# Routed attention and two feed-forward stages: number copies moved to the last products, four output buffers at first, a joined pair of tiles, another PSUM bank

## Chip, cores and metric

One NeuronCore of one Trainium2 chip. The metric is device time in microseconds; the median of three runs of the kernel before is 1136.23 us (1136.13 to 1136.47).

## What is computed

Three stages, all in float32 accuracy (4 batches, 8 heads, 576 tokens, head size 64; 2304 tokens of 512 features):

```python
scores = scale * np.matmul(q, k.transpose(0, 1, 3, 2))      # keep the 32 largest of each row
attn = softmax over the kept scores; x = attn @ v            # 2304 x 512
logits = xn @ en.T / tau; expert_idx = argmax                # 8 experts
out[mask] = gate_w * (relu(x[mask] @ w1[e]) @ w2[e])         # w1 512 x 1024, w2 1024 x 512
h = out @ w_in                                               # 512 x 2048
y = (relu(h) + alpha * min(h, 0)) @ w_out                    # 2048 x 512
```

## The kernel before, in words

The program is written out by hand: each engine (TensorE is PE, VectorE DVE, ScalarE ACT, GpSimd POOL, and SyncE SP, which issues nearly all transfers) executes its instructions in the order in which the code names them.

**Attention** (to about 466 us of the span) works on tiles of 128 queries. Of its eight PSUM banks one, `own`, holds small words (row sums, logits, gates); two hold the tiles `pt0`, into which PE transposes; five hold scores and outputs. `drain` puts work for the next stage between the last attention tiles: the splits of the first six weight units of the first expert, the transposes of its first 216 tokens, and three of its eight hidden tiles ("ahead"). Then `batch_done` routes the last batch: DVE computes logits, the place of each token (`place`, lines 708 and 709, reads the counts from a `pt0` tile) and the gates (`gates`, 690 and 691, read `own`), and POOL scatters the tokens' rows, sorted by expert, to `xs` in DRAM, with the token's number in column 512.

**Experts** (`run`, to about 733 us): nine blocks of tokens, two of the first expert and one of each other. A block has eight hidden tiles (`hidden`, 12 matmuls each) and then four column tiles `dc` of 24 matmuls. A float32 product is three fp32r products (`mm3`, lines 1098 to 1100) of high and low halves. So every weight unit (512 KB, a `raw` buffer of four, filled by an SP transfer) is split: ACT copies it, rounded, into `wt` (line 1022), and DVE or POOL subtracts (1023). `tick` does one item of a list of such splits and sends loads three items ahead; w_in and w_out, which are float64, are converted by `wide` on DVE and POOL in between. `turn` transposes the rows of the next block with PE (`x_chunk`, 1090, two `xt` banks), and ACT and DVE split them (1092, 1093). `gate` (1082) scales those rows by their gate first. A finished column tile is copied to `y` (two buffers, 1236 and 1238) and stored to `yt`. For each block but the first, `load_rows` also copies the block's token numbers, 4 bytes each, from column 512 of `xs` to `idc` with an SP transfer (line 1071, DRAM to DRAM).

**Last products** (`last_products`): nine groups of 256 tokens, passed twice (k = 0 to 17), once for each half of the 2048 features. Each k computes eight feature tiles f0 to f7 (12 matmuls each) and mixes them (`MIXED`) with seven products of the group before, by a seven-product scheme for a 2 x 2 block matrix; k = 0 has no products in between. At f7 `halves` splits the next group's columns (1268, 1269). Products are stored to `yp` in the first pass and scattered to the output in the second, by the numbers read back from `idc`. `Experts.bank` gives six PSUM banks, `mm`; in the experts and the last products they and the two `xt` banks lie on the attention's banks.

Of the kernel before, what the change touches and what calls it, by code (L numbers as in the profile page):

```python
# [48 lines left out]
class Attention:  # L49
    def __init__(self, ctx, tc, q, k, v, sb, ident):  # L50
# [8 lines left out]
        self.new_po()  # L59
        self.new_s()  # L60

        self.bank = self.ps.tile([P, 512], F32, name="own")
# [444 lines left out]
class Router:  # L507
# [161 lines left out]
    def batch_done(self, b):  # L669
# [89 lines left out]
        if b == B - 1:  # L759
# [3 lines left out]
                lambda: self.last_dots(3), numbers] + ahead(2) + [last_copies, root] + first + [  # L763
                counts, lambda: self.splits.pop(0)()] + [low[f] for f in range(AHEAD) if AT[f] == 1] + norm + [exps] + ahead(3) + [
                low[f] for f in range(AHEAD) if AT[f] == 2] + [place]
# [100 lines left out]
GAT = 4  # L866
EARLY_POOL = (0, 2, 4, 5)
RANKS = (0, 0, 16, 0, 0, 0, 0, 13)
ROWS = (-1, 0, 1, 2, 3, 4, 5)
GAT0, XAT0 = 0, ((), (), (), (), (0, 1), (2,), (3,), ())  # L870
XAT = ((), (0, 1), (), (2, 3), (), (), (), ())
# [4 lines left out]
class Experts:  # L876
# [3 lines left out]
    def __init__(self, tc, w1, w2, w_in, w_out, wa, xp, ident, xs, yt, idc, yp, ro, out):  # L880
        self.tc, self.nc = tc, tc.nc
        self.w1, self.w2, self.w_in, self.w_out = w1, w2, w_in, w_out
        self.ident, self.xs, self.yt, self.idc, self.out = ident, xs, yt, idc, out
        self.ro, self.wa, self.xp, self.yp = ro, wa, xp, yp
        self.W, self.rv = {}, {}
        self.items, self.sent = [], 0
        self.h0, self.p0, self.behind, self.ahead_of = [], [], [], []
        self.columns = None

# [31 lines left out]
    def early(self, lent):  # L921
# [4 lines left out]
        for k in range(EARLY):  # L926
            self.fetch(raws[k], k)
        return [lambda k=k: self.split(k, raws[k]) for k in range(EARLY)]

# [127 lines left out]
    def load_rows(self, r, o, n):  # L1057
# [11 lines left out]
        if r or o:  # L1069
            src = self.xs[ds(e * NT + o, n), DM]  # L1070
            self.after(4, lambda: nc.sync.dma_start(ids.rearrange("(a b) -> a b", a=8),
                                                    src.rearrange("(a b) -> a b", a=8)))
        else:
# [73 lines left out]
    def run(self, ctx, alpha):  # L1147
# [36 lines left out]
        for i, (r, o, n) in enumerate(blocks):  # L1184
# [40 lines left out]
            for dc in range(4):  # L1225
                ps = self.bank()[:, :n]
                for f in range(8):
                    u = self.W[8 * r + 4 + f // 2]
                    c = slice((f % 2) * 512 + dc * P, (f % 2) * 512 + (dc + 1) * P)
                    self.mm3(ps, u[:, 0, c], u[:, 1, c], hT[f][:, 0, :n], hT[f][:, 1, :n], f == 0, f == 7)  # L1230
                    if f == 3:
                        self.tick(2 * dc, 8)
                        turn(2 * dc)
                y = self.wk.tile([P, 512], F32, name="y", bufs=2)
                if dc % 2:
                    nc.scalar.activation(y[:, :n], ps, AF.Copy)
                else:
                    nc.vector.tensor_copy(y[:, :n], ps)
                self.after(2, lambda r=r, o=o, n=n, dc=dc, y=y, base=base: self.put(r, nc.sync.dma_start(
                    self.yt[dc, :, ds(base + o, n)] if r else self.yt[dc, :, o:o + n], y[:, :n])))  # L1240
                self.tick(2 * dc + 1, 8)
                if nb:
                    if i == 0 and dc == GAT0:
                        for j in range(4):
                            self.gate(rows[0], j)
                    turn(2 * dc + 1)
            xT, rows = nx, rows[1:]
        self.last_products(xT, len(plan[-2]), len(plan[-1]))
# [24 lines left out]
    def last_products(self, t, n0, n1):  # L1273
# [19 lines left out]

        def first(k, t, f):
            h, g = divmod(k, ng)
            ps = self.bank()[:, :G2]
            fs = slice(f * P, (f + 1) * P)
            for d in range(4):
                w = self.V[d]
                self.mm3(ps, w[:, 0, fs], w[:, 1, fs], t[d][:, 0, :G2], t[d][:, 1, :G2], d == 0, d == 3)  # L1300
            gg = G[k % 2][f // 4][:, f % 4]
# [3 lines left out]
        def weights(k, f):  # L1305
            self.n = n1 if k else n0
            full = 8 * (ng - 2) if k else 6
            at = 8 * (k - 1) + f if k else f
            for at in {6: (-1,), 7: (at - 1, at)}.get(f, (at,)) if k else (at,):
# [12 lines left out]
        def sums(k):  # L1322
# [4 lines left out]
            v.tensor_tensor(a11, a12, s2, op=OP.subtract)  # L1327
            return s2

        def fetch(k, tt):  # L1330
# [92 lines left out]
        for k in range(last + 1):  # L1423
# [3 lines left out]
            for s in order:  # L1427
# [7 lines left out]
                f = int(s[1])  # L1435
                first(k, t, f)
                if f == 7:
                    if k < last:
                        t = self.halves(x)
                        x = self.load_columns((k + 2) % ng if k + 2 <= last else ng)  # L1440
                    s2 = sums(k)
                    if k == last:
                        split(6, s2, v)
                for action in RENEW.get((k, f), ()):
                    action()
                if k and f < 5:
                    m, i, j = ((6, 0, 0), (5, 1, 0), (4, 1, 1), (2, 0, 1), (3, 0, 0))[f]
                    split(m, s2 if m == 6 else quarter(p, i, j))
                if f == 0 and not k:
                    nc.sync.dma_start(ids, self.idc[:NT].rearrange("(t p) -> p t", p=P))  # L1450
                if f == 1 and k == 1:
                    v.tensor_copy(idi, ids)
                if f == 3:
                    split(1, quarter(k, 0, 0))
                if f == 4:
                    s3 = new()
                    v.tensor_tensor(s3, quarter(k, 0, 0), quarter(k, 1, 0), op=OP.subtract)  # L1457
                if f == 5:
                    split(7, s3)
# [271 lines left out]
def tile_kernel(ctx, tc, q, k, v, emb, tau, w1, w2, w_in, w_out, alpha, out):  # L1731
# [11 lines left out]
    with ExitStack() as c0:  # L1743
        wa = c0.enter_context(tc.tile_pool(name="wa", bufs=1))
        xp = c0.enter_context(tc.tile_pool(name="xp", bufs=1))
        with ExitStack() as c1:
# [33 lines left out]
            def ahead(f):  # L1780
# [3 lines left out]
                if f < AHEAD:  # L1784
                    ex.ahead(f, banks[f])
            banks, ro.ahead, ro.low_half, ro.splits = [], ahead, ex.ahead_low, splits

            def drain(i):

                if i == -9:  # L1790
# [3 lines left out]
                    splits.extend(ex.early(lent))  # L1794
                if i >= 1 and len(splits) > 1:
                    splits.pop(0)()
# [42 lines left out]
```

## Time and profile before

| | |
|---|---|
| median of 3 runs | 1136.23 us |
| the profiled execution: time, span | 1134.85 us, 1133.0 us |
| PE busy | 1071.7 us (95%) |
| DVE / ACT / POOL busy | 78% / 64% / 67% |
| DMA | 134.99 MB, mean 119 GB/s |
| mean granted TensorE clock | 0.990 |

A busy PE is not PE at its best, but where PE is idle or its clock is granted at half, the time can be read off directly: the timeline gives, for each instruction that had to wait, the idle time before it and what ended it. Clock 1.00 is 2.4 GHz, 0.50 is 1.2 GHz.

### The profile page before, as it was taken

What the parts mean: (1) busy time and instruction counts of PE and PEld (TensorE: products, weight loads), DVE (VectorE), ACT (ScalarE), POOL (GpSimd) and SP (SyncE); (2) the same over time, 40 slices, a digit from 0 to 9 for tenths busy, and PEclk for the clock granted to TensorE, in tenths of its full rate; (3) what the DMA queues carried; (4) which work ended last, traced back from release to release, by engine and by line L of the source; (5) the groups of instructions that cost most, each with busy time, mean ns of one, the idle gap of its engine ahead of it and who ended that gap; (6) DMA issues with size and microseconds to landing.
All of it is one profiled execution on the core that took longest, in us unless ns stands there. A gap on an engine that the chain in (4) does not pass through costs nothing. (4 is left out here: it accounts for less than half of the span.)

```text
span 1133.0 us, 27513 instructions
## 1 busy us (share of the span) xinstructions
PE 1071.7 (95%) x9529; PEld 1019.0 (90%) x9529; DVE 884.8 (78%) x3443; ACT 724.2 (64%) x1543; POOL 759.8 (67%) x810
## 2 busy tenths in 40 slices
PE   4999999989998998998999999999999999999996
PEld 3888888878887887998999999999999999999996
DVE  7999999989998999644567566687999988556555
ACT  5999999999999989543445555453333455344341
POOL 4999988999899988514344445344665696675674
PEclk8999999999999999899999999999999999999999
DMA  6455343443343324188677888223333212311301
GB/s 176 129 148 152 97 103 100 116 116 80 96 105 94 68 53 169 44 198 219 205 200 195 211 240 245 83 68 117 127 94 114 74 47 66 103 66 57 122 30 41
DMA packets 149531, 134.99 MB, mean 119 GB/s; under 512 B 95054, under 2 KB 117582, under 8 KB 149382
## 3 DMA queue, kind: packets, MB, share of 16 engines
q1 hardware_dynamic: 145942, 123.16, 40.2%
q0 software_dynamic: 2912, 9.46, 2.3%
q8 instruction: 77, 1.26, 0.5%
q14 instruction: 72, 0.59, 0.2%
q10 hardware_dynamic: 528, 0.52, 0.1%
HBM read 89.82 MB, written 33.92 MB: 109 GB/s over the span
## 5 line engine op out<-in xcount | busy, mean ns | idle before, releaser
L1099 PE MATMUL mm<-xT,wt 128*128 128x256 f32 (+7 forms) x852 | 246.9, 290 | 3.4 <-DVE xT L1269 2.2
L1098 PE MATMUL mm<-xT,wt 128*128 128x256 f32 (+7 forms) x852 | 246.3, 289 | 3.4 <-DVE xtail L691 1.4
L1100 PE MATMUL mm<-xT,wt 128*128 128x256 f32 (+7 forms) x852 | 245.9, 289 | 0.0
L301 POOL TENSOR_TENSOR sg<-ss,sg 128x576 f32<-128x576 f32 x143 | 202.8, 1421 | 29.9 <-ACT sg L290 28.3
L219 DVE MAX8 cand<-ss 128x8 f32<-128x96 f32 x864 | 211.3, 245 | 14.0 <-ACT ss L209 12.6
L1362 PE MATMUL mm<-wt,hT 128*128 128x256 f32 x1512 | 193.0, 281 | 0.2 <-POOL hT L1320 0.2
L1362 PEld LDWEIGHTS mm<-wt,hT 128*128 128x128 f32 x1512 | 184.6, 189 | 0.9 <-POOL hT L1320 0.6
L1098 PEld LDWEIGHTS mm<-xT,wt 128*128 128x128 f32 x852 | 161.3, 189 | 4.4 <-DVE y L1363 1.8
L1099 PEld LDWEIGHTS mm<-xT,wt 128*128 128x128 f32 x852 | 161.3, 189 | 4.2 <-DVE xT L1269 2.8
L1100 PEld LDWEIGHTS mm<-xT,wt 128*128 128x128 f32 x852 | 161.5, 190 | 0.0
L960 POOL TENSOR_TENSOR wf<-wa,raw 128x512 f32<-128x512 f32 x32 | 44.1, 1379 | 115.8 <-DVE raw L855 83.5
L1023 POOL TENSOR_TENSOR wt<-raw,wt 128x1024 fp32r<-128x1024 f32 x28 | 73.2, 2619 | 71.7 <-ACT wt L1022 71.4
L290 ACT ACTIVATE sg<-ss,w 128x576 f32<-128x576 f32 x144 | 117.0, 812 | 4.2 <-DVE w L232 4.0
L327 PE MATMUL pt<-away,pen 128*128 128x128 bf16 x576 | 106.2, 220 | 12.0 <-POOL pen L310 12.0
L295 ACT ACTIVATE e<-ss,sm 128x576 f32<-128x576 f32 x144 | 116.2, 807 | 0.0
L326 PE MATMUL pt<-ident,e 128*128 128x128 f32 x576 | 115.7, 279 | 0.2 <-ACT pT L346 0.2
L241 DVE MAX8 w<-sg 128x8 f32<-128x576 f32 x144 | 106.9, 742 | 4.5 <-POOL spacer L786 4.0
L209 ACT ACTIVATE ss<-s 128x576 f32<-128x576 f32 x144 | 99.3, 690 | 10.0 <-POOL mg L309 7.9
L197 PE MATMUL s<-kt,qq 64*128 64x144 f32 (+1 forms) x1280 | 98.3, 306 | 4.7 <-ACT ss L209 2.5
L197 PEld LDWEIGHTS s<-kt,qq 64*128 64x128 f32 (+1 forms) x1280 | 77.3, 181 | 20.5 <-issue 8.4
L360 PE MATMUL po<-va,pT 128*128 128x65 f32 (+1 forms) x640 | 86.5, 278 | 8.4 <-ACT pc L395 8.4
L360 PEld LDWEIGHTS po<-va,pT 128*128 128x128 f32 x640 | 77.7, 191 | 15.9 <-ACT pc L395 13.0
(290 smaller groups left out, 2763.4 us busy)
## 6 DMA issues: line engine op xcount, KB each, us to landing
raw<-in_moe_w SPq DMA_DIRECT2D x59, 512.0 KB
xr<-yt SPq DMA_DIRECT2D x17, 512.0 KB
qq<-qt SPq DMA_DIRECT2D x60, 144.0 KB
xs<-zeros SPq DMA_DIRECT2D x8, 1028.0 KB
raw<-in_moe_w_in SPq DMA_DIRECT2D x16, 512.0 KB
raw<-in_moe_w_out SPq DMA_DIRECT2D x16, 512.0 KB
yt<-zeros SPq DMA_DIRECT2D x8, 704.0 KB
rows<-in_q SPq DMA_DIRECT2D x32, 144.0 KB
```

Of the source, the lines that this page charges most:

```text
L197: nc.tensor.matmul(s[to, g, c * n:c * n + n], t["qq"][of, h, q0:q0 + m], t["k"][of, h * HALF + c * n:h * HALF + c * n + n], start=True, st ...
L219: blocks.append(lambda i=i: nc.vector.max(A.cand[:, i], A.ss[:, i * BW:(i + 1) * BW if i + 1 < KB else S]))
L241: fin = [lambda: nc.vector.max(C.w[:, 24:32], C.z), lambda: nc.vector.scalar_tensor_tensor(scr, self.vsel, C.c1, C.w[:, 23:32, None].to_br ...
L290: nc.scalar.activation(T.sg, T.ss, AF.Sign, bias=T.w[:, 23:24], scale=-ABOVE, accum_out=T.c1)
L295: nc.scalar.activation(T.e[:, self.place(T)], T.ss, AF.Exp, bias=T.sm[:, 0:1], scale=0.125)
L301: eng.tensor_tensor(T.z, T.ss, T.sg, op=OP.mult)
L326: nc.tensor.matmul(o, T.e[:, k:k + P], self.ident, is_transpose=True, start=True, stop=False)
L360: nc.tensor.matmul(o, T.pT[:, c], rhs, start=c + j % 2 == 0, stop=False)
L1098: nc.tensor.matmul(ps, wh, xh, start=first, stop=False)
L1099: nc.tensor.matmul(ps, wh, xl, start=False, stop=False)
L1100: nc.tensor.matmul(ps, wl, xh, start=False, stop=last)
L1362: nc.tensor.matmul(ps, a[:, x, c], b[:, y, c], start=c == r == 0, stop=c == 3 and r == 2)
```

## The change

- An extra `pt0` tile is named before `own`, so `own` moves from PSUM bank 5 to 7 and the two `pt0` buffers from 6 and 7 to 5 and 6. Bank 5 is the second `mm` bank in use after the attention (hidden tile 4 of the first block).
- The sixth early weight unit (number 5, in a lent buffer of the attention, `qq`) is split in `drain`, beside unit 3, and by DVE in place of POOL.
- The transposes of the second block's tokens move from the third column tile (after f3), its end and the fourth's f3 to the fourth tile: three at its f3, the last at its end.
- `turn` stands before `tick` in the column tiles of all blocks.
- The first block's third and fourth output tiles have buffers of their own (those of `wa`).
- The eight copies of token numbers are issued in the last products, one at f1 of k = 1 to 8; they are read back at f1 of k = 9 in place of k = 0.
- At k = 0, f6 and f7 are computed together: for each 128 of the 512 inputs both tiles' matmuls, so that an input tile is done with after a quarter of the pair; the next group's `halves` come before their evacuation, and the two weight items of k = 0 fall on f0 and f2 in place of f2 and f5.

```diff
         self.new_s()
+        self.ps.tile([P, 4, P], F32, name="pt0", bufs=2)
         self.bank = self.ps.tile([P, 512], F32, name="own")
...
-                counts, lambda: self.splits.pop(0)()] + [low[f] for f in range(AHEAD) if AT[f] == 1] + norm + [exps] + ahead(3) + [
+                counts] + [low[f] for f in range(AHEAD) if AT[f] == 1] + norm + [exps] + ahead(3) + [
...
-EARLY_POOL = (0, 2, 4, 5)
+EARLY_POOL = (0, 2, 4)
-GAT0, XAT0 = 0, ((), (), (), (), (0, 1), (2,), (3,), ())
+GAT0, XAT0 = 0, ((), (), (), (), (), (), (0, 1, 2), (3,))
...
-        return [lambda k=k: self.split(k, raws[k]) for k in range(EARLY)]
+        return [lambda k=k: self.split(k, raws[k]) for k in (0, 1, 2, 3, 5, 4)]
...
-            self.after(4, lambda: nc.sync.dma_start(ids.rearrange("(a b) -> a b", a=8),
-                                                    src.rearrange("(a b) -> a b", a=8)))
+            self.numbers.append(lambda: nc.sync.dma_start(ids.rearrange("(a b) -> a b", a=8),
+                                                          src.rearrange("(a b) -> a b", a=8)))
...
                     if f == 3:
+                        turn(2 * dc)
                         self.tick(2 * dc, 8)
-                        turn(2 * dc)
-                y = self.wk.tile([P, 512], F32, name="y", bufs=2)
+                y = self.wk.tile([P, 512], F32, name="y" if i or dc < 2 else "wa", bufs=2)
...
-                self.tick(2 * dc + 1, 8)
...
                     turn(2 * dc + 1)
+                self.tick(2 * dc + 1, 8)
...
+        def features(t, fs):
+            ps = [self.bank()[:, :G2] for _ in fs]
             for d in range(4):
                 w = self.V[d]
+                for f, p in zip(fs, ps):
+                    c = slice(f * P, (f + 1) * P)
+                    self.mm3(p, w[:, 0, c], w[:, 1, c], t[d][:, 0, :G2], t[d][:, 1, :G2], d == 0, d == 3)
+            return ps
...
-            full = 8 * (ng - 2) if k else 6
-            at = 8 * (k - 1) + f if k else f
+            full = 8 * (ng - 2) if k else 2
+            at = 8 * (k - 1) + f if k else {0: 0, 2: 1}.get(f, 2)
...
+                two = not k and f > 5
+                if not two:
+                    bend(k, f, features(t, (f,))[0])
+                elif f == 6:
+                    continue
+                else:
+                    pair = features(t, (6, 7))
                 if f == 7:
                     if k < last:
                         t = self.halves(x)
                         x = self.load_columns((k + 2) % ng if k + 2 <= last else ng)
+                    if two:
+                        for g, ps in zip((6, 7), pair):
+                            bend(k, g, ps)
+                        s3 = seventh(k)
                     s2 = sums(k)
...
-                if f == 0 and not k:
+                if f == 1 and k and self.numbers:
+                    self.numbers.pop(0)()
+                if f == 1 and k == ng:
                     nc.sync.dma_start(ids, self.idc[:NT].rearrange("(t p) -> p t", p=P))
-                if f == 1 and k == 1:
+                if f == 7 and k == ng:
                     v.tensor_copy(idi, ids)
...
-                if i >= 1 and len(splits) > 1:
+                for _ in range((0, 1, 1, 1, 2, 1)[i] if 0 < i < 6 else 0):
                     splits.pop(0)()
```

Three places show how the order moves. SP, from the end of the attention into the second block (`raw_8905` and `raw_8907` are units 6 and 7, `raw_9032` on the next expert's; `xr` the rows of a block; what each waits for stands in brackets). Before:

```order
L911 DMA raw_8905<-in_moe_w2 128x2x512 [waits DMAHW0_49,PE_49,Pool_49]
...
L911 DMA raw_8907<-in_moe_w2 128x2x512
...
L1064 DMA xr_8975<-xs_62 128x2x514 [waits DMAHW3_49,DMASW3_49]
...
L1071 DMA idc_64<-xs_62 256x1 [waits DMAHW4_49]
...
L911 DMA raw_9032<-in_moe_w1 128x1024 [waits DMAHW5_49]
L1239 DMA yt_63<-y_9104 128x216 [waits DMAHW6_49,DVE_49]
...
L911 DMA raw_9258<-in_moe_w1 128x1024 [waits DMAHW5_49]
...
L1071 DMA idc_64<-xs_62 408x1 [waits DMAHW6_49]
...
L911 DMA raw_9299<-in_moe_w1 128x1024 [waits DMAHW7_49,DVE_49]
```

and now:

```order
L912 DMA raw_8906<-in_moe_w2 128x2x512 [waits DMAHW0_49,PE_49]
...
L912 DMA raw_8908<-in_moe_w2 128x2x512
...
L1065 DMA xr_8976<-xs_62 128x2x514 [waits DMAHW3_49,DMASW3_49]
...
L912 DMA raw_9032<-in_moe_w1 128x1024 [waits DMAHW4_49]
L1240 DMA yt_63<-y_9104 128x216 [waits DMAHW5_49,DVE_49]
...
L912 DMA raw_9258<-in_moe_w1 128x1024 [waits DMAHW4_49]
...
L912 DMA raw_9298<-in_moe_w1 128x1024 [waits DMAHW5_49,DVE_49]
```

The copies to `idc` are gone from between the loads, and unit 6's load no longer waits for POOL.

ACT, in the column tiles of the second block (`wt<-raw` is the split of a weight unit, `xT<-xt` that of the next block's tokens). Before:

```order
L1022 ACTIVATE wt_9379<-raw_9299 128x1024
L1022 ACTIVATE wt_9415<-raw_9321 128x1024
L1092 ACTIVATE xT_9425<-xt_9420 128x408
L1092 ACTIVATE xT_9433<-xt_9428 128x408
L1236 ACTIVATE y_9462<-mm_9436 128x256
```

and now:

```order
L1023 ACTIVATE wt_9378<-raw_9298 128x1024
L1093 ACTIVATE xT_9419<-xt_9414 128x408
L1093 ACTIVATE xT_9427<-xt_9422 128x408
L1023 ACTIVATE wt_9430<-raw_9320 128x1024
L1237 ACTIVATE y_9461<-mm_9435 128x256
```

The tokens' halves stand ahead of the second weight unit.

ACT, at the end of k = 0 (1302 evacuates a feature tile, 1319 splits an operand of a product, 990 splits a weight block, 1268 the next group's columns). Before:

```order
L1302 ACTIVATE hT_11842<-mm_11928 128x256
L1319 ACTIVATE hT_11841<-wa_11926 128x512
L990 ACTIVATE wt_11734<-raw_11740 128x1024
L1302 ACTIVATE hT_11842<-mm_11947 128x256
L1302 ACTIVATE hT_11842<-mm_11962 128x256
L1268 ACTIVATE xT_11977<-xr_11481 128x256
L1268 ACTIVATE xT_11980<-xr_11481 128x256
```

and now:

```order
L1307 ACTIVATE hT_11835<-mm_11920 128x256
L1269 ACTIVATE xT_11961<-xr_11469 128x256
L1269 ACTIVATE xT_11964<-xr_11469 128x256
...
L1307 ACTIVATE hT_11835<-mm_11935 128x256
L1307 ACTIVATE hT_11835<-mm_11936 128x256
L1324 ACTIVATE hT_11834<-wa_11978 128x512
```

The columns' split follows f5 at once; the last two evacuations and one operand's split come after it.

## Rows read from the trace of the kernel before

**Rows 1.** The page's part 1: busy time, share of the span, instructions.

```profile
PE 1071.7 (95%) x9529; PEld 1019.0 (90%) x9529; DVE 884.8 (78%) x3443; ACT 724.2 (64%) x1543; POOL 759.8 (67%) x810
```

**Rows 2.** Windows (length; busy PE, PEld, DVE, ACT, POOL; PE clock; DMA share, GB/s).

```profile
524.00:733.00 209.00, 207.55 (x1440) 205.97 (x1440) 132.54 (x189) 100.25 (x169) 90.05 (x41) 1.00 0.73 201
...
748.00:1124.00 376.00, 373.49 (x3141) 371.50 (x3139) 285.81 (x489) 159.02 (x361) 241.85 (x194) 1.00 0.26 83
```

**Rows 3.** Timeline of PE: start, length, line, tiles [idle before, what ended it].

```profile
476.21 0.55 PE L1098 MATMUL mm<-xT,wt 128*128 128x216 f32 x1 [1.36 <-DVE xtail L691]
...
490.89 0.33 PE L1090 MATMUL xt<-ident,xr 128*128 128x128 f32 x1 [0.80 <-ACT xr L1082]
491.51 0.55 PE L1090 MATMUL xt<-ident,xr 128*128 128x128 f32 x3 [0.29 <-ACT xr L1082]
...
498.46 0.39 PE L1099 MATMUL mm<-xT,wt 128*128 128x256 f32 x1 [1.13 <-DVE xT L1093]
...
518.99 1.09 PE L1090 MATMUL xt<-ident,xr 112*128 112x112 f32 x8 [3.23 <-DVE xT L1093]
...
643.85 0.41 PE L1099 MATMUL mm<-hT,wt 128*128 128x304 f32 x1 [1.26 <-DVE hT L1194]
...
745.61 0.39 PE L1098 MATMUL mm<-xT,wt 128*128 128x256 f32 x1 [0.85 <-ACT xT L1268]
...
747.39 0.39 PE L1099 MATMUL mm<-xT,wt 128*128 128x256 f32 x1 [1.39 <-DVE xT L1269]
...
902.43 0.38 PE L1098 MATMUL mm<-xT,wt 128*128 128x256 f32 x1 [1.00 <-DVE y L1363]
```

**Rows 4.** Windows of 2 us after two of these stalls; the clock is third from last.

```profile
476.00:478.00 2.00, 1.79 (x8) 1.79 (x9) 1.83 (x15) 0.00 (x0) 1.15 (x3) 0.53 0.32 78
478.00:480.00 2.00, 2.00 (x14) 2.00 (x12) 1.13 (x7) 0.00 (x0) 1.56 (x4) 0.62 0.99 347
...
520.00:522.00 2.00, 2.00 (x13) 2.00 (x13) 1.90 (x4) 2.00 (x4) 0.36 (x1) 0.62 0.58 109
522.00:524.00 2.00, 2.00 (x12) 2.00 (x11) 2.00 (x4) 0.52 (x1) 1.34 (x2) 0.53 0.94 296
```

**Rows 5.** Timeline of DVE, the end of routing and the first block.

```profile
473.53 0.20 DVE L708 TENSOR_TENSOR own<-pt,run 128x40 f32<-128x40 f32 x1
...
476.03 0.13 DVE L691 RECIPROCAL xtail<-own 64x1 f32<-64x1 f32 x1
...
492.29 0.76 DVE L1093 TENSOR_TENSOR xT<-xt,xT 128x256 fp32r<-128x256 f32 x2 [5.53 <-ACT xT L1092]
497.69 0.38 DVE L1238 COPY y<-mm 128x216 f32<-128x216 f32 x1 [4.64 <-DMA yt<-y]
```

**Rows 6.** Timeline of ACT at four places.

```profile
472.51 1.05 ACT L1022 ACTIVATE wt<-qq 128x1024 fp32r<-128x1024 f32 x1
...
490.12 1.34 ACT L1082 ACTIVATE xr<-xr 128x512 f32<-128x512 f32 x2 [5.44 <-DMA xr<-xs]
...
516.86 1.06 ACT L1022 ACTIVATE wt<-raw 128x1024 fp32r<-128x1024 f32 x1 [1.78 <-DMA raw<-in_moe_w]
...
640.53 1.07 ACT L1022 ACTIVATE wt<-raw 128x1024 fp32r<-128x1024 f32 x1 [4.14 <-DMA raw<-in_moe_w]
```

**Rows 7.** DMA issues: the number copies.

```profile
L1071 SPq DMA_DIRECT2D idc<-xs x8: 613/839/1099, 486.9 to 684.3; - x8
```

**Rows 8.** Windows of 2 us behind the second (issued at 501.79) and the sixth (625.66).

```profile
508.00:510.00 2.00, 2.00 (x19) 2.00 (x19) 0.92 (x3) 2.00 (x4) 1.51 (x2) 1.00 0.02 8
510.00:512.00 2.00, 2.00 (x19) 2.00 (x19) 0.42 (x1) 0.74 (x2) 2.00 (x1) 1.00 0.76 7
...
634.00:636.00 2.00, 2.00 (x17) 2.00 (x16) 0.47 (x1) 0.75 (x3) 1.03 (x1) 1.00 0.22 23
```

**Rows 9.** Timeline of ACT in the last products: its longest wait for a store.

```profile
904.33 0.39 ACT L1370 ACTIVATE y<-mm 128x256 f32<-128x256 f32 x1 [3.38 <-DMA yp<-y]
```

**Rows 10.** A window of 20 us in the last products.

```profile
840.00:860.00 20.00, 20.00 (x171) 20.00 (x171) 19.25 (x33) 7.16 (x17) 13.62 (x11) 1.00 0.37 115
```

More of the change, by code (lines that the diff above doesn't have):

```diff
@@ L887, in __init__ @@
         self.h0, self.p0, self.behind, self.ahead_of = [], [], [], []
-        self.columns = None
+        self.columns, self.numbers = None, []
     def reg(self, ap, n):
@@ L1292, in last_products, with bend @@
         O, raws = {}, {}
[L1294 to L1297, printed above, removed]
+        def features(t, fs):
+            ps = [self.bank()[:, :G2] for _ in fs]
             for d in range(4):
                 w = self.V[d]
-                self.mm3(ps, w[:, 0, fs], w[:, 1, fs], t[d][:, 0, :G2], t[d][:, 1, :G2], d == 0, d == 3)
+                for f, p in zip(fs, ps):
+                    c = slice(f * P, (f + 1) * P)
+                    self.mm3(p, w[:, 0, c], w[:, 1, c], t[d][:, 0, :G2], t[d][:, 1, :G2], d == 0, d == 3)
+            return ps
+        def bend(k, f, ps):
+            h, g = divmod(k, ng)
             gg = G[k % 2][f // 4][:, f % 4]
@@ L1328, in sums, with seventh @@
             return s2
+        def seventh(k):
+            s3 = new()
+            v.tensor_tensor(s3, quarter(k, 0, 0), quarter(k, 1, 0), op=OP.subtract)
+            return s3
         def fetch(k, tt):
@@ L1435, in last_products @@
                 f = int(s[1])
-                first(k, t, f)
+                two = not k and f > 5
[5 more added lines that the diff above has]
+                    pair = features(t, (6, 7))
                 if f == 7:
@@ L1440, in last_products @@
                         x = self.load_columns((k + 2) % ng if k + 2 <= last else ng)
+                    if two:
+                        for g, ps in zip((6, 7), pair):
+                            bend(k, g, ps)
+                        s3 = seventh(k)
                     s2 = sums(k)
+                    if two:
+                        split(7, s3)
                     if k == last:
@@ L1454, in last_products @@
                     split(1, quarter(k, 0, 0))
[L1455 to L1458, printed above, removed]
+                if f == 4 and k:
+                    s3 = seventh(k)
+                if f == 5 and k:
                     split(7, s3)
@@ L1785, in ahead @@
                     ex.ahead(f, banks[f])
-            banks, ro.ahead, ro.low_half, ro.splits = [], ahead, ex.ahead_low, splits
+            banks, ro.ahead, ro.low_half = [], ahead, ex.ahead_low
             def drain(i):
```

## The prediction

> **What bounds the kernel now.** I read the page's busy times first: PE works 95% of the span and no other engine over 78% [rows 1]. Then the windows by stage: in the two long stages PE is busy for 207.55 of 209 us and for 373.49 of 376 [rows 2]. So nothing moves the end but what stops PE or slows it, and the third view is PE's own timeline, where each row carries the idle time before it and what ended it [rows 3]. The reader should see there that the stalls stand in a few places: the first block's f4, the transposes of the second and third blocks, one place in a later block, and the end of k = 0 in the last products. The fourth view is windows of 2 us around them: behind two stalls the granted clock falls to 0.53 to 0.62, toward the 1.2 GHz level, and such time counts double [rows 4]. Last come the timelines of DVE and ACT [rows 5, 6], for what PE waited for, and the DMA views [rows 7, 8].
>
> The sum is made on the profiled execution, 1134.85 us. The median of the runs is 1136.23, that is 1.38 more, which I add at the end. A measurement of this kernel can tell about 0.2% from no change, 2.3 us.
>
> **Part 1: the bank of the small words, and unit 5's split.** PE stalls 1.36 us at 476.21, before f4 of the first block [rows 3]. That tile's bank is `own`'s, and DVE's last read of `own`, the gates, ends at 476.03 + 0.13 = 476.16 [rows 5]. Now f4's bank held the counts, whose reader `place` ends by 473.73 [rows 5], before f4 is due at 476.21 − 1.36 = 474.85. The stall goes: −1.36. Behind it two windows have clocks of 0.53 and 0.62 [rows 4]; against 1.00 they lose 2 × 0.47 + 2 × 0.38 = 1.70 us. Without the stall PE has no reason to lose them: −1.70. The price: ACT's share of unit 5's split, 1.05 us from 472.51 [rows 6], moves into the last attention tiles, ahead of ACT work there on which PE's transposes wait. It costs between 0 (ACT idle there) and 1.05 (all of it on the path); I take the upper middle, 0.65, since ACT feeds PE directly at that point. DVE's half takes POOL's place, and unit 6's load no longer waits for POOL. **Part 1: −2.4** (−3.1 to −2.0).
>
> **Part 2: transposes of the second block later, four output buffers.** Removed are the stalls 0.80, 0.29 and 1.13 us, 2.22 in all [rows 3]. The first two wait for ACT's scaling of the rows by the gate, which itself waited 5.44 us for the rows to land [rows 6]. The third waits for DVE's half of the transposed rows, and DVE stood 4.64 us waiting for a store of `y` to free a buffer [rows 5]; two more buffers take that wait away. What is late next: one column tile is 24 matmuls, some 2.5 us by the 19 per 2 us of [rows 8], so PE now comes to the first transpose 2.5 later by its own work but 2.4 earlier by part 1, and the scaling ends where it did, at about 490.12 + 1.34 ÷ 2 = 490.8 for the first half. I keep 0.6 of a wait there, and 0.9 for the third transpose, which stands in one burst with the first two and needs one of two `xt` banks back from ACT and DVE (DVE's half alone is 0.38 [rows 5]). 2.22 − 1.5 gives **part 2: −0.7** (−2.2 if both covers hold, +1 if a new half-clock stretch of 1.7 starts here).
>
> **Part 3: `turn` before `tick`.** The largest stall, 3.23 us at 518.99 [rows 3], waits for an `xt` bank whose DVE half comes behind ACT's, and ACT had two weight splits in front, one of which waited 1.78 us for its load and began at 516.86 [rows 6]. With the halves ahead of that split, ACT can read the bank as soon as PE has filled it. −3.23, and the slow clock behind it, again 2 × 0.38 + 2 × 0.47 = 1.70 [rows 4], goes with it. What moves behind is the weight splits, by two halves of about half a microsecond each; their units feed matmuls of a later item, and if that cover were gone PE would lose up to 1 us a block. **Part 3: −4.9** (−4.9 to −2.5).
>
> **Part 4: no number copies among the experts.** Eight copies are issued from 486.9 to 684.3 [rows 7]. Some 6 to 10 us behind the second the queues move 8 and 7 GB/s, and as late behind the sixth 23 [rows 8], against 201 on average over the stage [rows 2]. After the sixth ACT waits 4.14 us for a weight load (at 640.53) and PE 1.26 for what hangs on it (at 643.85) [rows 3, 6]. With the copies gone the loads land some microseconds sooner: **−1.26** (0 to −1.3; there is no other stall of such size to take away).
>
> A rule speaks against this term. The Trainium skill, page "DMA: Bandwidth & Descriptors", section "Why small descriptors are slow (HBM only)", puts the price of a small packet at a fixed overhead of about three cycles and 32 bytes of metadata. As an estimate by that page, 408 numbers over 16 engines are some 26 packets each, far under a microsecond, so that removing them would free nothing: the sum would be 1.3 us smaller, about 1126.2. The windows of [rows 8] disagree, several microseconds at under a ninth of the mean rate.
>
> **Part 5: f6 and f7 of k = 0 together.** Removed: 0.85 and 1.39, where the first products' successor waits for ACT's and DVE's halves of the next columns [rows 3], 2.24 together. The joined pair lets the halves start after its first quarters, while PE still has 18 of 24 matmuls, about 1.9 us. The two weight items moved to f0 and f2 go onto ACT and POOL; I keep 0.3 for them. **−1.9** (−2.2 to −0.5). The stall of 1.00 at 902.43 [rows 3] stays. The copies in the last products stand on SP behind stores, at a DMA share of 0.26 [rows 2]: nothing, unless the second rival holds.
>
> **The sum.** −2.4 − 0.7 − 4.9 − 1.3 − 1.9 = −11.2. 1134.85 − 11.2 = 1123.6 by the profile, and 1.38 more as a median: **1125.0 us**.
>
> **The rivals.**
> - *Given back to the weight loads.* The experts' stage already moves 201 GB/s at a DMA share of 0.73 [rows 2], and ACT waits for loads in it [rows 6]. A PE that comes 5 us earlier asks for each weight 5 us earlier; if the loads don't follow, parts 3 and 4 return as waits for splits, later in the stage. That costs half to all of 4.9 + 1.3: 1128 to 1131, about 1130 in the middle of what may follow with part 2 lost as well. For it: the waits for loads [rows 6]. Against: eight stretches of some 6 us at a low rate go [rows 8]. Chance 0.19.
> - *Slower: number copies hold up the stores of the last products.* There the output buffers of ACT wait for stores, at most 3.38 us [rows 9], while DVE is busy for 19.25 of 20 us [rows 10] and could not take over. If a copy delays a store's landing by the 6 us that [rows 8] show, ACT waits 3.38 + 6 = 9.4. PE runs on meanwhile through about five tiles of 12 matmuls, 60 × 2 ÷ 19 = 6.3 us, until it needs the held bank: 9.4 − 6.3 = 3.1 us, eight times, +25: 1150. It decides from a delay of about 3 us on. Against it: the stage has a DMA share of 0.26 [rows 2], so the copy's share lies on idle queues. Chance 0.06.
> - *No net change*: each stall taken out returns one place later, as PE meets the next late piece of ACT or DVE; 1134 to 1138. Against: the waits of [rows 3] have different causes, and PE runs for up to 100 us between them. Chance 0.04.
> - *A part that doesn't do what it says*: f4 waits for DVE although the bank is another, because DVE's `place` comes later with the split in its way. Then part 1 gives +0.65 and not −2.4, and the time is 1128. This lies inside the forecast's range.
>
> **How the numbers follow.** Forecast 0.71, its likeliest time 1125.0. The better ends of the parts, −3.1 − 2.2 − 4.9 − 1.3 − 2.2 = −13.7, give 1122.5, and with the wait at 902.43 gone by chance 1121.5; I put the low end at 1121.5. The upper end takes in the first rival, to 1131. Outside lie the second and third rivals and a little of the first's tail, under 2 in 10. Faster than before by over 0.2% 0.90, within 0.2% 0.04, slower 0.06.
>
> **What would show it.** Right: PE has no wait on DVE at the first block's f4, and a clock of 1.00 from 476 on; at the second block's transposes waits of at most 0.6 and 0.9; none over 1 us for `xt` in the third block; no `idc` copy from 486 to 684 and no window under 30 GB/s behind where they stood; no wait at the end of k = 0. Wrong: longer waits of ACT for weight loads in the experts, waits of ACT over 6 us for stores of `yp`, or a half clock where it is now full.

## The result, and the profile after

The changed kernel takes 1122.82 us (median of 6 runs, 1121.75 to 1125.67) against 1136.18 us for the kernel before: a ratio of 0.9892, 95% interval 0.9873 to 0.9912. The forecast was 1125.0, in a range of 1121.5 to 1131.0. The profiled execution took 1121.75 us, its span is 1119.9 us, that is 13.1 less than that of before.

The page's first part and the windows of the two long stages answer to [rows 1, 2]; three windows of 2 us stand behind them (in the windows: length; busy PE, PEld, DVE, ACT, POOL; PE clock; DMA share, GB/s):

```profile
PE 1066.6 (95%) x9529; PEld 1015.6 (91%) x9529; DVE 878.1 (78%) x3444; ACT 726.0 (65%) x1543; POOL 758.4 (68%) x809
```

```profile
515.00:720.00 205.00, 205.00 (x1432) 204.64 (x1431) 127.24 (x191) 101.07 (x170) 91.36 (x42) 1.00 0.64 206
734.00:1110.00 376.00, 372.91 (x3132) 370.72 (x3130) 286.07 (x488) 159.94 (x362) 242.13 (x195) 1.00 0.35 83
475.00:477.00 2.00, 2.00 (x20) 2.00 (x20) 1.83 (x14) 1.65 (x3) 0.85 (x1) 1.00 0.01 4
477.00:479.00 2.00, 2.00 (x20) 2.00 (x20) 1.93 (x10) 1.08 (x2) 1.56 (x5) 1.00 0.35 132
...
504.00:506.00 2.00, 2.00 (x20) 2.00 (x19) 0.77 (x3) 2.00 (x4) 1.51 (x2) 1.00 0.00 0
```

PE's busy time fell by 5.1 us only, the span by 13.1: most of what went was idle time, and the half clock with it. Among the experts PE is now busy without a break, and behind f4 the clock is 1.00 where [rows 4] have 0.53 and 0.62. PE's timeline shows what is left of the stalls of [rows 3], and one that is new:

```profile
490.27 0.55 PE L1091 MATMUL xt<-ident,xr 128*128 128x128 f32 x3 [0.22 <-ACT xr L1083]
491.54 0.44 PE L1091 MATMUL xt<-ident,xr 128*128 128x128 f32 x2 [0.71 <-DVE xT L1094]
...
752.12 3.11 PE L1372 MATMUL mm<-wt,hT 128*128 128x256 f32 x24 [0.89 <-DVE y L1373]
...
888.76 0.39 PE L1099 MATMUL mm<-xT,wt 128*128 128x256 f32 x1 [1.05 <-DVE y L1373]
...
908.21 0.39 PE L1100 MATMUL mm<-xT,wt 128*128 128x256 f32 x1 [0.79 <-DVE xT L1270]
```

The first two stand at the second block's transposes, the third is the new one, at k = 1, and the last two were there before (1.00 and 0.79 us).

PE runs the same 9529 matmuls in all these kernels, and save for the transposes and f6 and f7 in the same order. So the stages can be compared by count: the table gives the time between the starts of two matmuls, in us, worked out from each trace (the number is the place in PE's order). Of the experiments it gives those told of below; "numbers back" is the changed kernel with the copies back among the experts, "numbers alone" the kernel before with only the copies moved.

| from matmul to matmul | before | after | own bank 5 | split undone | numbers back | numbers alone | `tick` first | old transposes | two `y` | pair undone |
|---|---|---|---|---|---|---|---|---|---|---|
| 4401 to 4501, end of attention | 10.16 | 10.63 | 10.62 | 10.16 | 10.63 | 10.16 | 10.62 | 10.63 | 10.63 | 10.62 |
| to 4611, f4 and behind | 15.36 | 12.19 | 12.70 | 16.37 | 12.19 | 16.63 | 12.18 | 12.19 | 12.19 | 12.19 |
| to 4731, transposes of block 2 | 16.73 | 15.23 | 15.33 | 14.79 | 15.14 | 14.31 | 15.30 | 20.02 | 18.07 | 15.29 |
| to 4851, transposes of block 3 | 18.96 | 13.91 | 13.91 | 13.91 | 18.93 | 14.29 | 15.05 | 13.91 | 13.91 | 13.90 |
| to 6301, rest of the experts | 210.40 | 207.47 | 207.47 | 207.47 | 217.05 | 207.47 | 207.49 | 207.47 | 207.47 | 207.47 |
| to 6401, k = 0 | 14.69 | 11.94 | 11.94 | 11.94 | 11.94 | 16.01 | 11.94 | 11.94 | 11.94 | 14.71 |
| to 6551, k = 1 | 17.71 | 19.18 | 19.23 | 19.19 | 19.20 | 17.71 | 19.20 | 19.19 | 19.18 | 17.72 |

In this table the stages that an edit doesn't touch agree within 0.1 us nearly everywhere, so one profile shows a step well; a whole run varies by some microseconds. The kernel before was run again beside each group of experiments, with medians from 1132.84 to 1136.87 us, so the ratios can be compared from run to run, and the bare medians less well. Before and after differ by +0.47, −3.17, −1.50, −5.05, −2.93, −2.75 and +1.47, in all −13.5; the rest of the program is equal within 0.2 us.

### The profile page after: what moved, and what is told of

It reads as the page before. It is cut to its first block, busy times and chain, and to the rows that moved or that the text cites. A ratio compares the mean times of both kernels' runs of the same rounds, so it can differ in the third digit from the quotient of the medians.

```text
span 1119.9 us, 27504 instructions
## 1 busy us (share of the span) xinstructions
PE 1066.6 (95%) x9529; PEld 1015.6 (91%) x9529; DVE 878.1 (78%) x3444; ACT 726.0 (65%) x1543; POOL 758.4 (68%) x809
## 5 line engine op out<-in xcount | busy, mean ns | idle before, releaser
L220 DVE MAX8 cand<-ss 128x8 f32<-128x96 f32 x864 | 210.7, 245 | 14.5 <-ACT ss L210 13.6
L961 POOL TENSOR_TENSOR wf<-wa,raw 128x512 f32<-128x512 f32 x32 | 48.9, 1527 | 115.4 <-DVE raw L856 81.3
L1024 POOL TENSOR_TENSOR wt<-raw,wt 128x1024 fp32r<-128x1024 f32 x28 | 68.6, 2450 | 60.2 <-ACT wt L1023 60.1
L361 PEld LDWEIGHTS po<-va,pT 128*128 128x128 f32 x640 | 77.7, 191 | 16.0 <-ACT pc L396 13.1
```

Of the source, the lines that this page charges most:

```text
L220: blocks.append(lambda i=i: nc.vector.max(A.cand[:, i], A.ss[:, i * BW:(i + 1) * BW if i + 1 < KB else S]))
L361: nc.tensor.matmul(o, T.pT[:, c], rhs, start=c + j % 2 == 0, stop=False)
```

## The experiments

**The bank alone undone.**

```diff
-        self.ps.tile([P, 4, P], F32, name="pt0", bufs=2)
```

> The changed kernel with `own` back in PSUM bank 5; the split of unit 5 stays where the change put it. Theory (the bank is the cause): the wait of PE for DVE's gates before f4 of the first block returns with about 1.4 us, and the granted clock behind it falls to 0.5 to 0.6 for some 3.4 us, so the program is 3.1 us longer than the changed kernel, near 1126. Rival (what removed the stall is the split moved out of the routing, so that DVE's gates come sooner): no wait at f4 or one under 0.5 us, and the time of the changed kernel.

1123.67 us; ratio to before 0.9914 (0.9884 to 0.9944). PE's timeline at f4, with `own` in bank 5 again:

```profile
475.14 0.37 PE L1098 MATMUL mm<-xT,wt 128*128 128x216 f32 x1 [0.26 <-DVE xtail L691]
```

0.26 us are left of 1.36, and no half clock follows: the rival is right. DVE's timeline shows why: the first two fences are of the kernel before (DVE, and POOL beside it), the third of this run:

```profile
474.70 1.32 DVE L754 CAST slot<-mrow 128x5 int32<-128x5 f32 x1
475.94 0.17 DVE L690 RECIPROCAL xb<-own 128x4 f32<-128x4 f32 x1
```

```profile
473.63 2.36 POOL L1023 TENSOR_TENSOR wt<-qq,wt 128x1024 fp32r<-128x1024 f32 x1 [0.97 <-ACT wt L1022]
```

```profile
474.73 0.16 DVE L754 CAST slot<-mrow 128x5 int32<-128x5 f32 x1
474.86 0.18 DVE L690 RECIPROCAL xb<-own 128x4 f32<-128x4 f32 x1
```

A cast of five numbers in each partition took 1.32 us while POOL subtracted a weight unit, and 0.16 without; it ended with POOL's instruction (476.02 and 475.99). That microsecond is what PE waited for at f4.

**The split alone undone.**

```diff
-EARLY_POOL = (0, 2, 4)
+EARLY_POOL = (0, 2, 4, 5)
...
-        return [lambda k=k: self.split(k, raws[k]) for k in (0, 1, 2, 3, 5, 4)]
+        return [lambda k=k: self.split(k, raws[k]) for k in range(EARLY)]
```

(and its place, back behind the counts)

> The changed kernel with the split of unit 5 back at the counts and on POOL; `own` stays in the new bank. Theory (bank and split are apart: the bank took the wait away, the split's move costs 0.5 us in the last attention tiles): no wait at f4, PE reaches the end of attention 0.5 us sooner, the time is 0.5 us shorter than the changed kernel or the same. Rival (the split had to move for f4 to find its bank free, since POOL's work slows DVE's routing): a wait of 0.5 us or more at f4 and a half clock behind it, 2 to 3 us longer than the changed kernel.

1123.87 us; ratio 0.9917 (0.9884 to 0.9950). The end of attention is 0.47 shorter, as in the kernel before: that is the price of the moved split. f4 doesn't wait, for its bank is another; but a wait follows later. ACT's and PE's timelines, and two windows:

```profile
478.88 1.06 ACT L1023 ACTIVATE wt<-raw 128x1024 fp32r<-128x1024 f32 x1 [4.64 <-DMA raw<-in_moe_w]
...
480.74 1.06 ACT L1023 ACTIVATE wt<-raw 128x1024 fp32r<-128x1024 f32 x1 [0.32 <-DMA raw<-in_moe_w]
```

```profile
481.55 0.36 PE L1100 MATMUL mm<-hT,wt 128*128 128x216 f32 x1 [0.89 <-issue]
...
483.40 0.37 PE L1100 MATMUL mm<-hT,wt 128*128 128x216 f32 x1 [0.93 <-DVE hT L1195]
```

```profile
484.00:486.00 2.00, 2.00 (x10) 2.00 (x11) 1.39 (x13) 0.00 (x0) 0.00 (x0) 0.56 0.00 0
486.00:488.00 2.00, 2.00 (x13) 2.00 (x12) 0.00 (x0) 0.00 (x0) 0.00 (x0) 0.59 0.94 207
```

Unit 6's load is sent only when POOL is done with the buffer (SP issues it at 475.05 here, at 469.04 in the changed kernel), lands late, and PE stops twice, with the half clock behind it: 4.2 us by the table. So neither theory nor rival holds as written: the place of the wait is unit 6, not f4. In the changed kernel the split's move carries part 1, and the bank is worth 0.5 us. With the split at its old place the bank shows no gain: this stage takes 16.37 us here, 15.36 in the kernel before and 16.63 there with the copies alone moved. The medians of this run and of the one above can't be told from the changed kernel's; the prices are those of the table.

**The number copies back among the experts**, once and twice.

```diff
-            self.numbers.append(lambda: nc.sync.dma_start(ids.rearrange("(a b) -> a b", a=8),
+            self.after(4, lambda: nc.sync.dma_start(ids.rearrange("(a b) -> a b", a=8),
```

> The changed kernel with the eight copies of token numbers back among the experts' loads (read back still at k = 9). Theory (the copies hold up the weight loads behind them): windows under 50 GB/s return some 6 us behind each, ACT waits for a weight load by several us at least once, and PE loses 1.3 to 3 us in the experts' stage: 1124 to 1126. Rival (the copies are small packets of no weight, the loss near 644 came from something else of the change, such as `turn` before `tick`): no wait of PE in that stage and the time of the changed kernel.

> As the run before, but each copy of token numbers is issued twice among the experts' loads. It tells dose from chance: if the copies hold up the loads (theory), the low stretches become about twice as long (12 us for 6) and PE loses at least twice as much as in the run with single copies, 5 to 20 us. If it is the single small transfer that costs nothing and the loss is by chance of arrival (rival), the time stays within 1 us of that run.

Once: 1137.52 us (1131.46 to 1142.65, 10 runs), ratio to before 1.0031 (1.0003 to 1.0059): the whole gain is gone, with all other parts in place, where a loss of 1.3 to 3 us was expected. Twice: 1201.46 us, ratio 1.0586 (1.0541 to 1.0631), and not the 5 to 20 us expected. The stall behind the second copy, and windows of 2 us around it, in the run with single copies:

```profile
509.70 0.38 PE L1099 MATMUL mm<-hT,wt 128*128 128x256 f32 x1 [2.90 <-ACT hT L1194]
```

```profile
506.00:508.00 2.00, 0.81 (x7) 0.60 (x6) 0.20 (x1) 0.04 (x1) 0.00 (x0) 1.00 0.68 64
508.00:510.00 2.00, 0.30 (x1) 0.19 (x1) 0.32 (x1) 1.68 (x3) 0.55 (x1) 1.00 0.62 62
```

The queue moves 62 to 64 GB/s (8, 7 and 23 in [rows 8]), and PE stands. The view of waits names it for the whole stage (us waited in total, times, longest). ACT for weight loads, from 490 us to the experts' end, in the kernel before, the changed kernel, the copies back once, and twice:

```profile
ACT wt L1022 <- DMA raw<-in_moe_w: 28.1, 17, 4.1
```

```profile
ACT wt L1023 <- DMA raw<-in_moe_w: 7.7, 8, 4.1
```

```profile
ACT wt L1023 <- DMA raw<-in_moe_w: 41.3, 21, 5.6
```

```profile
ACT wt L1023 <- DMA raw<-in_moe_w: 83.4, 13, 11.8
```

**What of the copy it is.** Eight transfers in the old places that carry as many bytes to the same place in DRAM, from a source in one piece:

```diff
+            line = self.alpha_in[:n].rearrange("(a b) -> a b", a=8)
+            self.after(4, lambda: nc.sync.dma_start(ids.rearrange("(a b) -> a b", a=8), line))
```

> The changed kernel, with an extra transfer in each of the eight old places of the number copies: as many bytes from DRAM to the same place in DRAM, but from a source in one piece, so that the words are not gathered (the copies proper still follow in the last products). Theory (what costs is the gathering of 4-byte words, some 400 of them for each copy): no loss, within 1 us of the changed kernel. Rival (any small transfer from DRAM to DRAM there holds the loads up): most of the 14 us that the copies cost when they stood there.

1124.33 us (1122.41 to 1126.36), ratio 0.9910 (0.9890 to 0.9930); by the count of matmuls its profile is within 0.4 us of the changed kernel over every stage of the table. ACT's line in the same view:

```profile
ACT wt L1023 <- DMA raw<-in_moe_w: 10.1, 7, 4.6
```

So a transfer there costs nothing; gathering the words, 4 bytes each, does. In the trace's packet records of 498 to 520 us, the run with single copies has 580 packets of 4 bytes (192 in the changed kernel), of 11 ns in the mean, 6.2 us in all, shared by 16 engines; but the longest packet of a weight's 2 KB takes 5.1 us, against 0.7 in the changed kernel. By time, 444 of the 4-byte packets start from 502 to 504 us, and the loads' packets of over 1.5 us from 504.2 to 508.6. In the kernel before it is the same: after the copy issued at 501.79, 436 packets of 4 bytes start from 506 to 507, and 4 KB packets of a load that start at 507.5 to 507.6 take up to 5.4 us. The 4-byte packets are cheap by their own time, and the loads' packets behind them are long. Whether it is their number or the distance of the words in the source that does it was not tried.

**The copies moved, and nothing else**, in the kernel before:

```diff
-            self.after(4, lambda: nc.sync.dma_start(ids.rearrange("(a b) -> a b", a=8),
+            self.numbers.append(lambda: nc.sync.dma_start(ids.rearrange("(a b) -> a b", a=8),
```

> The kernel before, with the copies of token numbers moved to the last products and read back at k = 9, and nothing else changed. If the copies cost only what PE lost from 524 us on, up to the last products (theory of the prediction, by the steps of the two traces 2.9 us), 3 us less than the kernel before. If they were behind the stall at 519 too (rival), 8 us less, and that stall is gone or under 0.5 us with `tick` still first. If they cost nothing (the rule on small packets), the time of the kernel before.

1127.71 us (1126.31 to 1128.76), ratio 0.9922 (0.9895 to 0.9948): about 9 us, some seven tenths of the gain, and near the 8 us of the rival. The stall of 3.23 us in [rows 3] is gone though `tick` still stands first. At the second block's transposes one wait is left, and DVE's copy of `y`, which waited 4.64 us for a store in [rows 5], waits for PE alone; PE's and DVE's timelines there:

```profile
490.73 0.55 PE L1090 MATMUL xt<-ident,xr 128*128 128x128 f32 x3 [0.28 <-ACT xr L1082]
```

```profile
492.65 0.38 DVE L1238 COPY y<-mm 128x216 f32<-128x216 f32 x1 [0.38 <-PE mm L1100]
```

By the table it gains 2.42, 4.67 and 2.93 us in the three stages from the second block's transposes to the experts' end, and loses 1.3 each at f4 and at k = 0. Both losses are half clock: the stalls are those of the kernel before (1.36 us; 0.86 and 1.38), but the granted clock behind them is 0.50 from 476 to 480 and from 738 to 740, where the kernel before has 0.53 and 0.62 at f4 and 1.00 before k = 1. And of the 2.42 us, 1.3 only make up for f4: PE comes that much later to rows that land when they did.

**`tick` before `turn` again.**

```diff
-                        turn(2 * dc)
                         self.tick(2 * dc, 8)
+                        turn(2 * dc)
```

(and so at the column tile's end)

> The changed kernel with `tick` before `turn` again. Theory (the order on ACT is what took the 3.23 us stall and its half clock away): PE waits 2 to 3 us for an `xt` bank in the second block and the time is about 5 us longer than the changed kernel, 1128. Rival (that stall hung on a weight load that came late behind a copy of numbers, as the run with the copies put back suggests, which lost 4.9 us at the same place with `turn` first): with the copies gone the load is there, no wait over 0.5 us, and the time of the changed kernel, 1122 to 1124.

1122.70 us, ratio 0.9887 (0.9853 to 0.9921): nearer the rival. Of the 3.23 us a wait of 0.83 comes back:

```profile
511.61 1.09 PE L1091 MATMUL xt<-ident,xr 112*128 112x112 f32 x8 [0.83 <-DVE xT L1094]
```

With the loads on time the order of the two is worth 1.14 us by the table, not 5, and nothing that a median shows.

**The second block's transposes at their old places; and two output buffers.**

```diff
-GAT0, XAT0 = 0, ((), (), (), (), (), (), (0, 1, 2), (3,))
+GAT0, XAT0 = 0, ((), (), (), (), (0, 1), (2,), (3,), ())
```

> The changed kernel with the second block's transposes at their old places (two after f3 of the third column tile, one at its end, one after the fourth's f3); the four output buffers stay. Theory (the later place hides the wait for the rows): waits of about 1 us for ACT's scaled rows return, no wait for the third transpose, 0.4 us longer than the changed kernel, and 2 us if the clock falls to half behind it. Rival (the place is worth nothing, since the rows land sooner now): waits under 0.3 us, and up to 0.7 us shorter than the changed kernel.

```diff
-                y = self.wk.tile([P, 512], F32, name="y" if i or dc < 2 else "wa", bufs=2)
+                y = self.wk.tile([P, 512], F32, name="y", bufs=2)
```

> The changed kernel with two output buffers for the first block again; the later transposes stay. Theory (a store's landing held DVE up, and with it the halves the next block waits for): DVE waits some 4 us for a store of `y`, PE about 1 us at the second block's first tile, 1 us longer than the changed kernel. Rival (that store was late behind the first copy of numbers, as 1.1 us of PE's wait went in the kernel before with the copies moved alone): no wait, and the time of the changed kernel.

Old places: 1127.31 us, ratio 0.9907 (0.9879 to 0.9936), by the table 4.8 us longer in this stage (its profiled execution lost another 4 us early in the attention, where the edit changes nothing). Two buffers: 1124.62, ratio 0.9910 (0.9891 to 0.9928), 2.8 longer. In the first ACT waits for the rows and PE for ACT, and the clock behind is 0.50:

```profile
495.17 1.33 ACT L1083 ACTIVATE xr<-xr 128x512 f32<-128x512 f32 x2 [8.38 <-DMA xr<-xs]
```

```profile
495.95 1.52 PE L1091 MATMUL xt<-ident,xr 128*128 128x128 f32 x4 [2.84 <-ACT xr L1083]
```

```profile
498.00:500.00 2.00, 2.00 (x12) 2.00 (x11) 0.35 (x1) 0.00 (x0) 0.00 (x0) 0.50 0.03 6
```

In the second DVE's copy of `y` waits for a store, and the halves behind it hold an `xt` bank:

```profile
492.32 0.38 DVE L1239 COPY y<-mm 128x216 f32<-128x216 f32 x1 [8.44 <-DMA yt<-y]
```

```profile
493.09 0.69 PE L1091 MATMUL xt<-ident,xr 128*128 128x128 f32 x2 [1.93 <-DVE xT L1094]
```

Both edits are worth more than expected. Counted from matmul 4401, part 1 brings PE to matmul 4611 2.7 us sooner than in the kernel before (22.8 us in place of 25.5), while ACT has the rows only 0.7 us sooner in the first of these runs (26.9 in place of 27.6). That the wait for the store grows for the same reason is likely, but not shown apart. Neither rival holds.

**f6 and f7 of k = 0 apart**, with the weight items at their old places:

```diff
-                two = not k and f > 5
+                two = False
...
-                if f == 4 and k:
+                if f == 4:
                     s3 = seventh(k)
-                if f == 5 and k:
+                if f == 5:
                     split(7, s3)
```

> The changed kernel with f6 and f7 of k = 0 apart and the weight items at f2 and f5, as before. Theory (the pair took away 2.7 us at k = 0, of which DVE's later work at k = 1 takes 1.3 us back): the two waits before k = 1 return with 0.9 and 1.4 us, the wait of 0.9 us at k = 1 goes, net 1.3 us longer than the changed kernel. Rival (the two waits came of PE's place relative to ACT, which the earlier parts shifted): waits under 0.5 us at both places and the time within 0.5 us.

1125.55 us, ratio 0.9908 (0.9879 to 0.9938). Both waits come back as they were, and the one of 0.89 at k = 1 goes:

```profile
732.64 0.38 PE L1099 MATMUL mm<-xT,wt 128*128 128x256 f32 x1 [0.85 <-ACT xT L1269]
...
734.41 0.38 PE L1100 MATMUL mm<-xT,wt 128*128 128x256 f32 x1 [1.39 <-DVE xT L1270]
```

2.77 longer at k = 0 and 1.46 shorter at k = 1: net 1.31, as the theory has it.

**DVE's pieces later**, an attempt to beat the changed kernel, in two runs; the second has the right k, and unit 5's split one step later.

```diff
-                if f == 4 and k:
+                if f == 4 and k > 1:
                     s3 = seventh(k)
                 if f == 5 and k:
+                    if k == 1:
+                        s3 = seventh(k)
```

```diff
-                weights(k, f)
+                if f < 7 or k != ng - 2:
+                    weights(k, f)
...
                         product(p, s)
+                        if k == ng - 2 and s == 3:
+                            weights(k, 7)
```

> The changed kernel with two pieces of DVE's work later: at k = 1 the operand of the seventh product is formed after f5 and not after f4, and the weight item at the end of k = 8 stands behind the three products there. Theory (the waits of 0.9 and 1.05 us at 752 and 889 are for output tiles that wait in DVE's queue behind these pieces): both waits fall under 0.3 us, 1.5 to 2 us shorter than the changed kernel, 1121. Rival (DVE's whole work of that stretch is too long, so the wait moves to the next tile): the same sum of waits, some us later, and the same time.

> As the run before with DVE's pieces later, but the second piece moved at the right place: the wait at 889 stands at the end of k = 7, not of k = 8, so the weight item of k = 7 goes behind the three products there. And unit 5 is split one step later in the last attention tiles. Theory (each of the three delays is work of DVE or ACT that stands ahead of what PE waits for): no wait over 0.3 us at 752 and at 888, and PE reaches the end of the attention 0.5 us sooner; 1.8 + 0.5 us less than the changed kernel, 1120.5. Rival (the work only moves): the wait of 1.0 us comes back at the start of k = 8, and the later split holds up the first hidden tiles by 1 us instead; the time of the changed kernel.

1122.22 us, ratio 0.9890 (0.9873 to 0.9906), and 1122.90, 0.9890 (0.9856 to 0.9925): not to be told from the changed kernel. In both the wait at 752 is gone (1.13 us less at k = 1). In the first the wait at 888 stays, for it stands at the end of k = 7 and the piece was moved at k = 8. In the second it goes, but a longer one takes its place; PE's and POOL's timelines:

```profile
891.60 1.45 PE L1372 MATMUL mm<-wt,hT 128*128 128x256 f32 x10 [2.25 <-POOL hT L1325]
```

```profile
888.02 1.32 POOL L961 TENSOR_TENSOR wf<-wa,raw 128x512 f32<-128x512 f32 x1 [6.85 <-DVE raw L856]
889.30 2.25 POOL L1325 TENSOR_TENSOR hT<-wa,hT 128x512 fp32r<-128x512 f32 x1
```

DVE's later piece makes POOL's conversion later, and with it POOL's half of a product's operand. The later split of unit 5 changed nothing (the end of attention took 10.61 us).

## Why the prediction was right, and where it was not

The time and the direction were right, and the sum of −11.2 is near the −13.5 that the steps show. Its causes were right in part only, and that parts 1 and 3 came out near their size is luck: their stalls went with another edit than the one named, and that edit stood in the same change.

- **Part 1** (−2.4): −2.70 by the steps (+0.47 and −3.17; the price was put at 0.65). But the step "now f4's bank held the counts, so the stall goes" names the wrong edit: with the bank undone 0.5 us come back. The work that made the gates late was DVE's cast of 1.32 us beside POOL's subtraction, which my sum did not price; moving that split, to an earlier place and onto DVE, was the cure (which of the two does it was not tried apart). It also frees unit 6's load, which the prediction told of and put at nothing; the split put back costs 4.2 us there.
- **Part 2** (−0.7): −1.50. The wait of 0.6 for the scaled rows was 0.22, and the third transpose waits 0.71, near the 0.9 kept. The stall of 1.13 was put down to the number of output buffers; in the kernel before it went with the copies alone, as the store then landed in time. What was not seen either is that without these two edits the gain of part 1 would have been lost here: 4.8 and 2.8 us.
- **Part 3** (−4.9): −5.05 at that place, but the step "with the halves ahead of that split" is not what did it. The copies moved alone take 4.67 us away there; with the copies back the stage takes 18.93 us though `turn` stands first; and with the loads on time the order is worth 1.14. The reading stopped at ACT's row in [rows 6], which waited 1.78 us for a load, and didn't ask why that load was late: the copy issued at 501.79, whose windows stood in [rows 8].
- **Part 4** (−1.3): −2.93 in its own stage. When the copies alone were moved, 10.0 us went in this and the two stages before it, 8.7 without what only made up for f4, and 9 in the median. This is the term mis-sized most: the eight copies were priced by the one stall of PE that stood behind a late load after the sixth. The estimate worked out from the Trainium skill's page "DMA: Bandwidth & Descriptors", section "Why small descriptors are slow (HBM only)", had the removal worth nothing; the small price of a packet that the Trainium skill gives there is borne out (11 ns for 4 bytes), and the estimate is not, since the time goes in the loads' packets behind. One sign did not hold, "no window under 30 GB/s behind where they stood": from 504 to 506 the changed kernel moves 0 GB/s, at a DMA share of 0.00 and with PE busy throughout. There no load is under way; so a low rate alone doesn't tell that a load is held up, and the time of its packets does.
- **Part 5** (−1.9): −2.75 at k = 0, and +1.47 back at k = 1, net −1.28. PE comes to k = 1 sooner, and an output tile there waits in DVE's queue behind the operand of the seventh product: with that operand formed later, 1.13 us came back. What the moved weight items, for which 0.3 had been kept, have in it was not tried.

Of the rivals, "given back to the weight loads" did not come: ACT's waits for loads fell from 28.1 to 7.7 us. Nor did the slower one: in the last products the view of waits has, where [rows 9] had 3.38 as the longest,

```profile
ACT y L1380 <- DMA yp<-y: 3.0, 2, 2.4
```

though the copies stand there; the one whose landing the trace has took 9.3 us. They lengthen packets here too: the longest 4 KB packet of this stage takes 8.8 us, against 1.2 in the kernel before, and the DMA share rises from 0.26 to 0.35 at the same 83 GB/s. But nothing is near enough to wait for what they hold up.

Two readings in the prediction are slightly off and change nothing: `place` reads the counts until 473.92 with its second line, not 473.73, and 23 GB/s is a little over a ninth of 201.

What stays open: why the loads' packets behind the gathered words take so long, and why the copies put back cost 9.6 us in the rest of the experts' stage in the changed kernel and 2.9 in the kernel before. PE comes to each weight sooner in the one; that this is the reason was not tried.

## What to carry to other kernels

Where an engine waits for a load, look at what the queues did in the microseconds before it, and not only at the order of the engine's own queue: here one cause stood behind three stalls that looked like three. Gathers of single words belong where no load is urgent. And a gain early in the program has to be followed to the next piece that was just in time: the prediction had 0.7 us for the later transposes and the extra buffers, and without either of them the gain of part 1 would have been lost.

## What the runs showed that was not expected

- Copies of 256 to 408 words of 4 bytes cost more the more of them there are, out of proportion: eight copies 14.5 us by the steps in the changed kernel, sixteen 79 us. As many bytes from a source in one piece cost nothing.
- DVE's cast of 128 x 5 numbers took 1.32 us beside a POOL subtraction of 2.36 us, and 0.16 us without it. It was so in all three kernels in which POOL subtracts there (1.32, 1.35 and 1.32 us), while DVE's other small instructions in the same stretch kept their 0.2 us.
- The half clock behind one and the same stall differs from kernel to kernel: behind the two waits before k = 1 (0.85 and 1.39 us) the kernel before has 1.00, and with the copies alone moved, behind waits of 0.86 and 1.38, a window at 0.50.
